# One weight unit made wholly resident in a segment-recurrent attention kernel, with its scratch homes shared

## The chip, the core and the metric

The kernel runs on one core of a Trainium2 chip. Its engines are TensorE (PE in the profile, with its weight loads as PEld), VectorE (DVE), ScalarE (ACT), GpSimd (POOL) and SyncE (SP); 16 DMA engines move data between HBM and the on-chip memory SBUF. TensorE accumulates in PSUM, which has eight banks. The metric is the device time of one execution in microseconds (us), as the median of several runs.

## The reference

Two branches read the same normalised rows `xn` of `x` (2048 rows of 1024): a feed-forward branch with a GELU over 3584 columns, and an attention that walks through the rows in 64 segments of 32, each together with eight memory rows. The first eight output rows of a segment are the memory of the next, so the segments form a chain.

```python
def _A_ref(x, mem0, Wq, Wk, Wv, Wo, seg_len):
    ...
    for s in range(n_seg):
        xs = x[:, s * seg_len:(s + 1) * seg_len, :].copy()
        h = jnp.concatenate([mem, xs], axis=1)
        q = jnp.einsum('btd,dhe->bhte', h, Wq)
        k = jnp.einsum('btd,dhe->bhte', h, Wk)
        v = jnp.einsum('btd,dhe->bhte', h, Wv)
        scores = jnp.einsum('bhqe,bhke->bhqk', q, k) * scale
        scores = jnp.where(mask[None, None], scores, -1000000000.0)
        p = _softmax(scores, axis=-1)
        o = jnp.einsum('bhqk,bhke->bhqe', p, v)
        o = jnp.einsum('bhte,hed->btd', o, Wo)
        mem = o[:, :M, :].copy()
        outs.append(o[:, M:, :])
    return jnp.concatenate(outs, axis=1)
...
xn = _layernorm(x, axis=-1)
return x + _A_ref(xn, ...) + _B_ref(xn, B_w1, B_b1, B_w2, B_b2)
```

There are 32 heads of 128. Each of the four weights Wq, Wk, Wv and Wo has 1024 x 4096 elements of bf16.

## The kernel before

**Phases.** The first 416 us compute the normalised rows, their transposes and the whole feed-forward branch, and put `x` plus that branch back to HBM as a residual (`R_n`, and from there, laid out for the segments, into the second half of `hr_d` and `hrL_d`). Then the segment loop runs 64 times.

**Units.** The attention's weights are cut into 64 units of 128 x 2048 elements (512 KB). A segment takes them in the order of `pass_order`: half passes K0, Q0, K1, Q1, V0, V1 of eight units each (0 and 1 are the two halves of the heads), then pass O with 16. A unit of the six half passes is four matmuls of 512 columns side by side, one in each group of 32 columns of the array (`product`, L774); pass O is `o_product` (L1010).

**Resident and streamed.** 46 units lie in SBUF for good, in places that the feed-forward branch gave up (`RES_PLACES`), in the `late` pool (`LATE`), or in `xt2` and `xt3`. 18 units (an "S" in `PLACED`) are streamed again in each segment through a ring of six slots (`RING`). When a streamed unit is done, `unit_done` calls `start_stream`, which fills the freed slot with the next unit in order. Three of the 18 are special. `IN_PSUM` (the second streamed unit of Q0) and `IN_BANKS` (the last unit of pass O) are kept in four PSUM banks and copied to their slot by DVE (L271, two instructions of 512 words each); they are started three places late (`LATER`). `PART` is the streamed unit third from the end of the streamed units of pass O (O's unit 11): its first 1792 of 2048 columns lie in `half_home`, and only 256 columns (512 B in each of 128 rows, 64 KB) are streamed into its slot (L282). All other transfers of a unit are whole (L284). SP issues them all.

**The scores.** Within a segment the attention of head half `u` is: `scores(u)` on TensorE into the bank `mixed` (L884, L890), `exps(u)` (ACT's Exp into `pr`, L899, then two masks on DVE, L906), `sums(u)` (sums on TensorE L914 and L920, then Ln and two Exp on ACT, L925 and L928, then two products on DVE, L937 and L941, into `pdA` and `pdB`), and `values(u)` on TensorE (L956, L962) with four copies out (L975). They are put between the units of later half passes by unit number: `scores(0)` after the last unit of K1, `sums(0)` after unit 4 of Q1 (`SUMS_0`), `scores(1)` with `exps(1)` after unit 0 of V1 (`ATTEND`), `values(0)` around unit 4 of V1, `sums(1)` after unit 5 or 6 of V1, and `values(1)` after unit 5 of O. The queries of both halves use one home, `q_home` (a view of `q_all`): `turn_q` copies them out of PSUM with ACT (L826) and transposes them in place with DVE (L840). `q_left` puts the queries of left rows beside them (L862).

**Homes.** `pr_all` holds pr of both halves. `pdB` of half 0 lies in `res_home`, the second half of `hr_home`; `pdB` of half 1 at the end of `q_all`. `hr_home` also receives the rows of the next segment (first half) and the residual of the running one (second half): from segment 6 on one transfer of 1 KB rows brings both, behind V1 (L293, on POOL). Before that, ACT issues the two separately.

**Left rows.** Each segment owns 24 rows and its eight memory rows in the main products; eight "left" rows of four segments each are collected and computed together. So the segments differ by `i4 = s % 4`: left keys in the K passes, left queries in Q and left values in V are added in some of them, and in those with `i4 == 1` (`left_o`) pass O has the left rows as well. `left_outs` and `left_keys` are interleaved in two homes, `ko_flat`.

**The end of a segment.** `put_mem` (L320, L330) turns the first output rows into the next segment's memory rows; then DVE adds the residual (L1178), and the output goes out with four small transfers (L1213), from POOL from segment 5 on. All engines run their instructions in program order; dependences become semaphore waits.

Of the kernel before, what the change touches and what calls it, by code (L numbers as in the profile page):

```python
# [10 lines left out]
BF16 = mybir.dt.bfloat16  # L11
# [35 lines left out]
STREAMED = 18  # L47
# [16 lines left out]
AT_BANKS, AT_PART = 5, 3  # L64
PART_COLS = 1792


def pass_order():
# [15 lines left out]
    "S..S...." "S...S..." "S....S.." ".S.....S" "....S..." "S..S..S." "...S..S." "S..S..SS",  # L84
    "S..S...." "S...S..." "S....S.." ".S.....S" "....S..." "S..S..S." "...S..S." "S..S..SS",
    "S..S...." "S...S..." "S....S.." ".S.....S" "....S..." "S..S..S." "...S..S." "S..S..SS",
    "S..S...." "S...S..." "S....S.." ".S.....S" "....S..." "S..S..S." "...S..S." "S..S..SS",
# [21 lines left out]
IN_BANKS, PART = STREAMED_O[AT_BANKS], STREAMED_O[AT_PART]  # L109
# [5 lines left out]
def kernel(  # L115
# [34 lines left out]
    hr_d = dram.tile([NSEG + 1, P, 512], BF16, name="hr_d")  # L150
    hrL_d = dram.tile([NGRP + 1, P, 512], BF16, name="hrL_d")
# [12 lines left out]

    half_home = nc.alloc_sbuf_tensor_at("half_home", [P, PART_COLS], BF16, offset=SCRATCH)

    part_home = half_home[:, :]
# [5 lines left out]
    hr_home = consts.tile([P, 512], BF16, name="hr_home")  # L173
    res_home = hr_home[:, 256:512]
    pr_all = consts.tile([P, 224], BF16, name="pr_all")
    pd_main = consts.tile([P, 320], BF16, name="pd_main")
# [9 lines left out]
    qL_last = consts.tile([P, 16, SEG], BF16, name="qL_last")  # L186
    qL = [consts.tile([P, 16, SEG], BF16, name="qL"), qL_last]
    ident = res_home[:, 0:P]
    make_identity(nc, ident)
    ident_mem = nc.alloc_sbuf_tensor_at("ident_mem", [P, 4, NL], BF16, offset=SCRATCH + 2 * PART_COLS)  # L190
# [9 lines left out]
    mask = qL_last.rearrange("p h t -> p (h t)")[:, 0:NX + GRP * 16]  # L200
# [29 lines left out]
    for k in range(7):  # L230
# [8 lines left out]
        unit: dram.tile([P, 2048 - PART_COLS if unit == PART else 2048], BF16, name="Wc_" + "_".join(map(str, unit)))[:, :]  # L239
# [3 lines left out]
    def fetch(t, unit):  # L243
        w, i, u = unit
        if unit == PART:
            h = 4 * i + 2 * u
            nc.sync.dma_start(out=t, in_=Wo_v[:, h + 1, PART_COLS - DM:])
        elif w == "O":
# [24 lines left out]
    def start_stream(slot):  # L273
# [7 lines left out]
        elif unit == PART:  # L281
            nc.sync.dma_start(out=t[:, PART_COLS:], in_=copies[unit])  # L282
# [8 lines left out]
    def load_x_rows(s, eng=nc.sync):  # L291
        n = 512 if s > 5 else 256
        eng.dma_start(out=hr_home[:, 0:n], in_=hr_d[s, :, 0:n])  # L293
        nxt["hT"] = hr_home[:, 0:256].rearrange("p (k t) -> p k t", k=KT)

    def load_left_rows(g, eng=nc.sync):
        hr = hrp.tile([P, 256], BF16, name="hrL")
        eng.dma_start(out=hr[:, :], in_=hrL_d[g, :, 0:256])
# [6 lines left out]
    ko_flat = [d_oL[:, 512:], sp.tile([P, 16 * 48], BF16, name="ko1")[:, :]]  # L305
    ko = [t.rearrange("p (h t) -> p h t", h=16) for t in ko_flat]
    left_outs, left_keys = [t[:, :, 0:SEG] for t in ko], [t[:, :, 2 * NL:] for t in ko]
    q_all = sp.tile([P, 640], BF16, name="q_all")
# [28 lines left out]
    with tc.tile_pool(name="ma", bufs=2) as ma, tc.tile_pool(name="mps", bufs=6, space=PSUM) as mps:  # L337
# [95 lines left out]
        def keep_xT(tg, xnT):  # L433
            xl = [t[:, 0:512].rearrange("p (g k i t) -> p g k i t", g=2, k=KT, i=GRP) for t in ko_flat]
            for half in range(2):
                nc.sync.dma_start(
                    out=hr_d[16 * tg:16 * tg + 16, :, 128 * half:128 * half + 128].rearrange("s p c -> p s c"),
# [7 lines left out]
            for k in range(2):  # L445
                nc.sync.dma_start(
                    out=hrL_d[4 * tg + 2 * k:4 * tg + 2 * k + 2, :, 0:256].rearrange("g p c -> p g c"),
# [15 lines left out]
        def turn_R(ttg, eng, small=None):  # L463
# [3 lines left out]
            for i in range(4):  # L467
# [4 lines left out]
                    t[:, 256:512].rearrange("(h r) c -> r h c", h=2)  # L472
                    for t in (hr_d[min(4 * og + 1, NSEG - 1) + 1, :, :], hrL_d[og, :, :])
# [5 lines left out]
                else:  # L479
                    pairs = [(hr_d[seg + 1, :, 256:512].rearrange("(j t) c -> t j c", j=4), rows)]  # L480
# [69 lines left out]
        for tg in range(4):  # L550
            last = tg == 3
            if last:
# [4 lines left out]
                nc.sync.dma_start(out=half_home[:, 0:DM], in_=Wo_v[:, h, :])  # L557
# [122 lines left out]
    with tc.tile_pool(name="late", bufs=1) as late, \  # L680
# [67 lines left out]
        for s in range(NSEG):  # L748
# [101 lines left out]
            def turn_q(ps):  # L850
                turn(ps, q_home[:, :, NL:40], nc.scalar.copy)
# [399 lines left out]
```

## Time and profile before

| what | value |
|---|---|
| median of 3 runs (lowest to highest) | 1830.54 us (1828.19 to 1836.0) |
| profiled execution, its own time | 1831.03 us |
| its span, instructions | 1828.9 us, 71537 |
| granted TensorE clock | 0.999 |
| busy PE, DVE, ACT, POOL | 1723.1, 959.5, 670.1, 269.3 us |
| moved by DMA | 596.27 MB |
| first and last `put_mem` matmul (L320) | 449.9 and 1801.3 us |

Between the first and the last `put_mem` lie 62 segments. The page's slices divide the span in 40 equal parts of 45.7 us; the loop begins in the tenth. A wait line gives the engine and line that waited, what released it, and then the total in us, how often, and the longest. A timeline line gives start and length in us, engine, line, operation, output and input.

### The profile page before, as it was taken

The page shows a single profiled execution, that of the slowest core. Times are in us where ns is not written, and L with a number is a line of the kernel's source. Part 1 is how long each engine was busy: PE and PEld are TensorE (multiplying, and loading weights), DVE is VectorE, ACT ScalarE, POOL GpSimd, SP SyncE. Part 2 cuts the span into 40 slices and gives each one's busy share as a digit, 9 for nine tenths or more (in the row PEclk, how much of TensorE's full clock was granted, in tenths as well). Part 3 has the DMA queues.
Part 4 walks back from the last instruction along what each step waited for, and adds up shares of the span by engine and source line. Part 5 has one row for each costly group of instructions (what it writes and reads, how often), then busy time and mean ns, then how long its engine had stood idle before and what let it go on. Part 6 is the DMA issues. An engine that isn't in the chain of part 4 may idle for free.

```text
span 1828.9 us, 71537 instructions
## 1 busy us (share of the span) xinstructions
PE 1723.1 (94%) x31207; PEld 873.1 (48%) x31207; DVE 959.5 (52%) x2443; ACT 670.1 (37%) x1572; POOL 269.3 (15%) x526
## 2 busy tenths in 40 slices
PE   8999999998999999999999999999999999999987
PEld 4444444444444445454445544454444444445444
DVE  7657483805455545455555555555555454545544
ACT  5334251602333334333333333333333333333333
POOL 0000001501231111111111111111111111111111
PEclk9999999999999999999999999999999999999999
DMA  9931211769999999999999999999999999999997
GB/s 290 314 88 48 53 46 49 252 221 362 379 385 378 377 371 386 373 389 367 388 384 377 401 375 380 379 380 376 380 372 385 374 374 376 370 393 395 369 379 304
DMA packets 230662, 596.27 MB, mean 326 GB/s; under 512 B 46411, under 2 KB 86107, under 8 KB 230348
## 3 DMA queue, kind: packets, MB, share of 16 engines
q1 hardware_dynamic: 207028, 571.28, 83.8%
q0 software_dynamic: 15872, 16.44, 2.8%
q8 instruction: 244, 4.00, 0.9%
q10 hardware_dynamic: 7448, 3.98, 0.7%
q14 instruction: 70, 0.57, 0.1%
HBM read 577.63 MB, written 28.97 MB: 332 GB/s over the span
## 4 chain that ended last, share of the span: by engine, by line
PE 65%; DMA 30%; issue 2%; DVE 1%; ACT 1%; SPq 0%; ACTq 0%; POOL 0%; DVEq 0%; POOLq 0%
PE acc L774 29%; DMA u<-Wc_V 13%; PE ps L503 11%; PE acc L1010 10%; PE ps L624 8%; DMA u<-Wc_O 7%; DMA u<-Wc_Q 5%; DMA u<-Wc_K 3%; PE ps L657 2%; PE acc L956 2%; DMA hr_home<-hr_d 1%; DVE u L271 1%; PE pT L657 1%; PE mixed L320 0%; PE mixed L884 0%
## 5 line engine op out<-in xcount | busy, mean ns | idle before, releaser
L774 PE MATMUL acc<-u,hr_home 128*32 128x512 bf16 x11520 | 793.4, 380 | 52.7 <-DMA u<-Wc_V 24.7
L774 PEld LDWEIGHTS <-hr_home 128*32 128x32 bf16 x12288 | 327.9, 96 | 374.5 <-issue 70.2
L774 PE MATMUL acc<-u,hrL 128*32 128x512 bf16 x2880 | 250.4, 380 | 1.7 <-issue 1.5
L503 PE MATMUL ps<-u 128*128 128x512 bf16 (+1 forms) x920 | 195.7, 375 | 2.0 <-ACT u L423 2.0
L271 DVE TENSOR_SCALAR u<-kept 128x512 uint32<-128x512 uint32 x254 | 163.5, 685 | 60.0 <-PE acc L1010 38.3
L826 ACT CAST d_oL<-acc 128x512 bf16<-128x512 f32 x143 | 82.0, 586 | 270.5 <-PE acc L774 258.4
L624 PE MATMUL ps<-u 128*128 128x512 bf16 x672 | 147.0, 379 | 0.0
L503 PEld LDWEIGHTS <-u 128*128 128x128 bf16 x920 | 90.5, 99 | 105.4 <-issue 2.4
L1010 PE MATMUL acc<-u,q_all 128*32 128x256 bf16 (+1 forms) x2096 | 126.5, 301 | 14.7 <-DMA u<-Wc_O 10.9
L1010 PE MATMUL acc<-u,d_oL 128*32 128x512 bf16 x1944 | 133.6, 381 | 7.1 <-DMA u<-Wc_O 4.1
L937 DVE TENSOR_TENSOR pd_main<-pr_all,mixed 128x320 bf16<-128x320 bf16 x128 | 62.5, 488 | 126.9 <-ACT mixed L928 125.3
L830 ACT CAST q_all<-acc 128x512 bf16<-128x512 f32 x128 | 75.4, 589 | 144.1 <-PE mixed L890 141.0
L840 DVE STREAM_TRANSPOSE q_all<-q_all 128x512 bf16<-128x512 bf16 x128 | 90.6, 708 | 70.7 <-ACT q_all L826 70.7
L1010 PEld LDWEIGHTS <-q_all 128*32 128x32 bf16 x3381 | 102.0, 96 | 53.6 <-ACT q_all L975 23.2
L1213 POOL DMA_DIRECT2D out_dram<-hr_home x172 | 88.1, 512 | 243.1 <-DVE hr_home L1178 237.7
L293 POOL DMA_DIRECT2D hr_home<-hr_d x58 | 32.9, 567 | 594.9 <-PE acc L774 581.7
L826 ACT CAST q_all<-acc 128x512 bf16<-128x512 f32 x128 | 75.3, 589 | 93.4 <-PE acc L774 93.4
L774 PEld LDWEIGHTS <-hrL 128*32 128x32 bf16 x3072 | 83.4, 96 | 48.1 <-issue 2.8
L624 PEld LDWEIGHTS <-u 128*128 128x128 bf16 x672 | 65.3, 98 | 77.3 <-DVE g_u L585 0.4
L1010 PEld LDWEIGHTS <-d_oL 128*32 128x32 bf16 x2592 | 67.7, 96 | 62.6 <-issue 15.0
L928 ACT ACTIVATE mixed<-mixed,small_consts 128x160 f32<-128x160 f32 x256 | 94.4, 369 | 8.4
L577 ACT ACTIVATE g_xb<-ps,b1col 128x512 bf16<-128x512 f32 x112 | 76.9, 687 | 55.3 <-PE ps L503 54.5
(139 smaller groups left out, 2094.5 us busy)
## 6 DMA issues: line engine op xcount, KB each, us to landing
u<-Wc_K SPq DMA_DIRECT2D x256, 512.0 KB
u<-Wc_V SPq DMA_DIRECT2D x256, 512.0 KB
u<-Wc_O SPq DMA_DIRECT2D x256, 512.0 KB
u<-Wc_Q SPq DMA_DIRECT2D x192, 512.0 KB
u<-in_B_w_dram SPq DMA_DIRECT2D x28, 512.0 KB
hr_home<-hr_d POOLq DMA_DIRECT2D x58, 128.0 KB, 5.3
u<-in_A_Wq_dram SPq DMA_DIRECT2D x13, 512.0 KB
u<-in_A_Wv_dram SPq DMA_DIRECT2D x12, 512.0 KB
```

Source lines behind the costliest of these rows:

```text
L271: nc.vector.tensor_single_scalar(out=out, in_=in_, scalar=0, op=ALU.bitwise_or)
L503: nc.tensor.matmul(ps[:, SEG * s0:SEG * s1].rearrange("p (s t) -> p s t", t=SEG), lhsT=w1_sb[fb // 2][:, kt, (fb % 2) * P:(fb % 2 + 1) * P ...
L577: nc.scalar.activation(out=xb[:, :], in_=ps[:, :], func=ACT.Identity, bias=b1col[:, fb:fb + 1], scale=1.0)
L624: nc.tensor.matmul(ps[:, :], lhsT=gts[fc // 4][:, fc % 4, t * P:(t + 1) * P], rhs=w2_sb[fc // 2][:, fc % 2, cs], start=(fc == 0), stop=(fc ...
L774: nc.tensor.matmul(o, lhsT=lhs[:, i, :], rhs=m, start=(i == seq[0]), stop=(i == seq[-1]), tile_position=(0, 32 * j),)
L826: cp(out=out, in_=ps.rearrange("p (h e) -> p h e", e=32))
L830: cp(out=t[:, :], in_=ps[:, :])
L840: nc.vector.transpose(out=home, in_=home)
L928: nc.scalar.activation(out=mixed[:, 160 * b:160 * b + 160], in_=mixed[:, 0:160], func=ACT.Exp, scale=-1.0, bias=off[:, b:b + 1],)
L937: nc.vector.tensor_tensor(out=pdA.rearrange("p c b q -> p b c q"), in0=prA[:, None, :, :].to_broadcast([P, 2, 4, 40]), in1=dd, op=ALU.mult,)
L1010: nc.tensor.matmul(acc[r0:r0 + rows, c:c + wide], lhsT=lhsT, skip_group_check=True, rhs=cols, start=start, stop=stop, tile_position=(0, r0),)
L1213: eng.dma_start(out=out_flat[rows, 256 * j:256 * j + 256], in_=res[32 * j:32 * j + NX, :])
```

## The change

O's unit 11 becomes resident as a whole: `STREAMED` is 17, the "S" at its place in `PLACED` becomes ".", it gets a place of its own in the `late` pool, and `PART`, `part_home` and the split of its columns in `o_columns` go. `IN_BANKS` is still the last unit of O. The 512 B in each partition come from sharing homes:

- `hr_home`, both `qL` and `pd_main` lie where `half_home` was; `pr_all` is gone.
- pr of half 0 lies in columns 400 to 623 of `q_all`, where the second queries will be; pr of half 1 lies in `res_home`.
- So `q_left(1)` moves from within `exps(0)` to behind `sums(0)`, and the copy of the second queries is cut in two at head 10 (column 400 of `q_all`).
- `pdB` of half 0 lies in a strided part of `left_outs`; its product is made in two instructions.
- The residual has DRAM tensors of its own (`res_d`, `resL_d`) and is loaded by itself after unit 0 of O, behind the products of `sums(1)`; the rows (`rows_d`, `rowsL_d`) are loaded where they were.
- `ko1` and `q_all` become parts of one tile `kq`, which also receives half of the banked unit at the start.

```diff
-STREAMED = 18
+STREAMED = 17
...
-AT_BANKS, AT_PART = 5, 3
-PART_COLS = 1792
+AT_BANKS = 4
...
-    "S..S...." "S...S..." "S....S.." ".S.....S" "....S..." "S..S..S." "...S..S." "S..S..SS",
+    "S..S...." "S...S..." "S....S.." ".S.....S" "....S..." "S..S..S." "...S..S." "S.....SS",
...
-    half_home = nc.alloc_sbuf_tensor_at("half_home", [P, PART_COLS], BF16, offset=SCRATCH)
+    hr_home = nc.alloc_sbuf_tensor_at("hr_home", [P, 512], BF16, offset=SCRATCH)[:, :]
+    qL = [
+        nc.alloc_sbuf_tensor_at(f"qL{u}", [P, 16, SEG], BF16, offset=SCRATCH + 1024 * (u + 1))[:, :, :] for u in range(2)
+    ]
+    pd_main = nc.alloc_sbuf_tensor_at("pd_main", [P, 320], BF16, offset=SCRATCH + 3072)[:, :]
...
-        elif unit == PART:
-            nc.sync.dma_start(out=t[:, PART_COLS:], in_=copies[unit])
...
     def load_x_rows(s, eng=nc.sync):
-        n = 512 if s > 5 else 256
-        eng.dma_start(out=hr_home[:, 0:n], in_=hr_d[s, :, 0:n])
+        eng.dma_start(out=hr_home[:, 0:256], in_=rows_d[s, :, :])
...
-            def turn_q(ps):
-                turn(ps, q_home[:, :, NL:40], nc.scalar.copy)
+            def turn_q(ps, cuts=(0, 16)):
+
+                for h0, h1 in zip(cuts, cuts[1:]):
+                    nc.scalar.copy(
+                        out=q_home[:, h0:h1, NL:40], in_=ps[:, 32 * h0:32 * h1].rearrange("p (h e) -> p h e", e=32)
+                    )
+                let_go(ps)
+                home = q_home[:, :, NL:40]
+                nc.vector.transpose(out=home, in_=home)
...
-            def exps(u, meanwhile=None):
+            def exps(u):
 
-                pr = pr_all[:, 0:224]
+                pr = res_home[:, 0:224] if u else q_all[:, 400:624]
...
-                if meanwhile is not None:
-                    meanwhile()
...
-                pdB = (q_all[:, 512:640] if u else res_home[:, 0:128]).rearrange(
-                    "p (c b a q) -> p c b a q", c=4, b=2, q=NL
-                )
+                if u:
+                    pdB = q_all[:, 512:640].rearrange("p (c b a q) -> p c b a q", c=4, b=2, q=NL)
+                else:
+                    c0 = 0 if first else NL * slot
+                    pdB = left_outs[1 if first or i4 >= 2 else 0][:, :, c0:c0 + NL].rearrange(
+                        "p (c b a) q -> p c b a q", c=4, b=2
+                    )
...
+                else:
+                    for a in range(2):
+                        nc.vector.tensor_tensor(
+                            out=pdB[:, :, :, a, :].rearrange("p c b q -> p b c q"),
+                            in0=prB[:, None, :, NL * a:NL * a + NL].to_broadcast([P, 2, 4, NL]),
+                            in1=dd[:, :, :, 32 * a:32 * a + NL], op=ALU.mult,
+                        )
...
-            exps(0, None if first else lambda: q_left(1))
+            exps(0)
...
-            if not first:
-                at[SUMS_0[i4]] = [lambda: sums(0)]
+            at[7 if first else SUMS_0[i4]] = [lambda: sums(0)] + ([] if first else [lambda: q_left(1)])
...
-            turn_q(psQ1)
+            turn_q(psQ1, (0, 10, 16))
...
             def load_res():
                 st["res"] = res_home
-                if s < 5:
-                    nc.scalar.dma_start(out=res_home, in_=hr_d[s + 1, :, 256:512])
+                (nc.scalar if s < 5 else nc.gpsimd).dma_start(out=res_home, in_=res_d[s + 1, :, :])
...
             if not final:
                 load_x_rows(s + 1, nc.scalar if s < 5 else nc.gpsimd)
-            else:
-                nc.gpsimd.dma_start(out=res_home, in_=hr_d[s + 1, :, 256:512])
```

More of the change, by code (lines that the diff above doesn't have):

```diff
@@ L244, in fetch @@
         w, i, u = unit
[L245 to L248, printed above, removed]
+        if w == "O":
             h = 4 * i + 2 * u
```

100 lines of the change are left out of this document (45 added, 55 removed).

## The prediction

> **What bounds the kernel now.** I read the page's slices first, then its chain, then the waits of TensorE, then windows of 1 us, and last the timeline of one segment. The slices show the 16 DMA engines at nine tenths or more all through the segment loop (from slice 10 on), at 367 to 401 GB/s in most slices; the chain that ended last runs through TensorE and, for nearly a third of the span, through the transfers of streamed weights.
>
> ```profile
> DMA  9931211769999999999999999999999999999997
> GB/s 290 314 88 48 53 46 49 252 221 362 379 385 378 377 371 386 373 389 367 388 384 377 401 375 380 379 380 376 380 372 385 374 374 376 370 393 395 369 379 304
> ...
> PE 65%; DMA 30%; issue 2%; DVE 1%; ACT 1%; SPq 0%; ACTq 0%; POOL 0%; DVEq 0%; POOLq 0%
> ```
>
> The waits of TensorE (total us, times, longest) are few and small, and nearly all are for streamed units:
>
> ```profile
> PE acc L774 <- DMA u<-Wc_V: 24.7, 56, 1.8
> PE acc L1010 <- DMA u<-Wc_O: 15.0, 28, 1.4
> PE acc L774 <- DMA u<-Wc_Q: 11.6, 19, 1.7
> PE acc L774 <- DMA u<-Wc_K: 4.3, 7, 1.7
> ```
>
> That is 55.6 us, the most that a better stream can give. The loop is balanced: some 62 segments in 1351 us (21.8 us each), with under 1 us of DMA wait in each. I call a segment s of kind s mod 4. Kind 1 projects the left rows in pass O as well; there TensorE is slow and the ring fills. The windows (the last two columns are DMA share and GB/s) cross from a kind 1 into the next segment:
>
> ```profile
> 1165.00:1166.00 1.00, 1.00 (x28) 0.49 (x20) 0.35 (x2) 0.25 (x1) 0.57 (x1) 1.00 1.03 397
> ...
> 1167.00:1168.00 1.00, 1.00 (x26) 0.65 (x22) 0.45 (x1) 0.00 (x0) 0.00 (x0) 1.00 0.95 332
> 1168.00:1169.00 1.00, 1.00 (x28) 0.48 (x20) 0.00 (x0) 0.00 (x0) 0.00 (x0) 1.00 0.93 299
> 1169.00:1170.00 1.00, 1.00 (x23) 0.36 (x16) 0.00 (x0) 0.59 (x1) 0.00 (x0) 1.00 0.79 274
> ...
> 1179.00:1180.00 1.00, 1.00 (x24) 0.57 (x17) 0.53 (x2) 0.59 (x1) 0.00 (x0) 1.00 1.03 422
> ```
>
> For about ten of each 87 us (four segments) the transfers are short of work and TensorE is the bound; in the rest the transfers are, and TensorE meets their delay in V, O and Q.
>
> **Part 1, the bytes.** In each of segments 1 to 63 the 64 KB of the partly resident unit are not streamed; in segment 0 the same 512 KB are fetched either way. 65,536 B at 380 GB/s are 0.17 us. The queue table gives the same from the other side:
>
> ```profile
> q0 software_dynamic: 15872, 16.44, 2.8%
> ...
> q10 hardware_dynamic: 7448, 3.98, 0.7%
> ```
>
> The ACT queue's packets average 534 B and take 0.007 x 1828.9 x 16 / 7448 = 27.5 ns; the POOL queue's average 1036 B and take 51.6 ns. The 128 rows of 512 B that go are 128 x 27.5 / 16 engines = 0.22 us. The residual loaded apart turns 128 rows of 1 KB into 256 of 512 B: 128 x (55.0 - 51.6) / 16 = 0.03 us more, and no more bytes. So 0.17 to 0.19 us; I take 0.17, and 63 x 0.17 = 10.7 us, of which 77/87 fall where transfers bind: **-9.5 us**. Bounds: -13.9 (0.22 everywhere) and 0 (TensorE the bound throughout).
>
> **Part 2, the ring.** With 17 places in the stream and six slots, a start happens when the unit six places before is done. The dropped place stands third from the end of pass O, so between the last unit of V0 and that place every start moves one streamed unit forward: the first of K1 starts when O's unit 8 is done and not at unit 11. The SP queue shows that start and the two before it:
>
> ```profile
> 1161.49 2.36 SPq L284 DMA_DIRECT2D u<-Wc_K  x2
> 1165.29 0.32 SPq L284 DMA_DIRECT2D u<-Wc_Q  x1
> 1167.47 1.60 SPq L284 DMA_DIRECT2D u<-Wc_K  x2
> ```
>
> Three units of O take some 1.3 us in kind 1 (the PE timeline steps 0.43 us a unit), so the start at 1167.47 comes at 1166.1, and the Q before it at about 1163.3. In the three windows from 1167 the engines moved 332, 299 and 274 GB/s and not 410, 0.33 MB or 0.8 us short. Half of that, 0.4 us in each of 16 rounds, is **-6.4 us**; bounds -13 and 0. Where transfers bind anyway, an earlier start only queues earlier. The copy of the banked unit on DVE also moves, from O's unit 8 to unit 6: 1.29 us of DVE work, in an idle stretch of DVE behind the two casts of `values`, costs nothing; were that cover gone it would delay the fold of L1031, which has until the end of O.
>
> **Part 3, the second queries' transposition.** pr of head half 0 now lies in q_all, so `q_left(1)` and the second piece of Q1's copy wait for `sums(0)`: Ln and two Exp on ACT, then the products on DVE. The timeline of a kind 1 before the change:
>
> ```profile
> 1156.50 0.59 ACT L826 CAST q_all<-acc 128x512 bf16<-128x512 f32 x1
> 1156.61 0.49 DVE L937 TENSOR_TENSOR pd_main<-pr_all,mixed 128x320 bf16<-128x320 bf16 x1 [0.94 <-ACT mixed L928]
> 1157.02 0.28 DVE L941 TENSOR_TENSOR hr_home<-pr_all,mixed 128x128 bf16<-128x128 bf16 x1
> 1157.21 0.70 DVE L840 STREAM_TRANSPOSE q_all<-q_all 128x512 bf16<-128x512 bf16 x1
> 1157.97 0.20 PE L884 MATMUL mixed<-q_all,d_oL 128*32 128x40 bf16 x4
> ```
>
> ACT's copy lay beside the products; the transposition followed them at once and ended at 1157.91, and `scores(1)` came 0.06 us later. Now: L941 for u = 0 becomes two instructions of 64 elements (DVE casts of 128x64 take 0.22 us and such pairs overlap by 0.08): 0.36 for 0.28, so +0.08. Then ACT's second piece, 192 columns: 0.21 us for 64 and 0.38 for 256 in L975's rows give 0.32. The overlap of 0.09 between product and transposition is lost, and two handovers come in at some 0.04 (ACT's end to DVE's start was 0.02 in L826 to L840 of Q0). Together +0.57 us on the transposition; if the piece also waits for `q_left(1)`'s copy (0.15), +0.72. Behind the waiting piece on ACT is only V0's copy, which needs `scores(1)` itself; behind the transposition on DVE the masks of pr(1). TensorE waits for both.
>
> Over all segments the transposition ended before `scores(1)` by, in the median, 1.57 us in kind 0, 0.30 in kind 1, 0.69 in kind 2 and 0.38 in kind 3. Taking 0.57 less each segment's own slack, where that is positive, gives 8.7 us over the loop; 2.1 of it stands within 4 us ahead of a DMA wait that it only replaces. Of the 6.6 left I take **+6 us**; bounds 0 (the stream absorbs it) and 14 (0.72, nothing absorbed).
>
> **Part 4, the residual.** It was in one transfer with the rows, behind V1. Now POOL issues it after the products of `sums(1)`, since pr(1) lies in its home. This row gives the landing:
>
> ```profile
> hr_home<-hr_d POOLq DMA_DIRECT2D x58, 128.0 KB, 5.3
> ```
>
> In kinds 0 and 3 those products end 4.3 us before `put_mem`, the add of L1178 stands 0.5 us after it: the data is late by about 0.5 us; in kind 2 by nothing, in kind 1 it is 2 us early. DVE has 0.35 us idle before the bank copy of L271 and 0.84 before K0's transposition, which cover it: **0 us**, bounds 0 and +6 (0.2 us in each of 31 segments). The Trainium skill, page "DMA: Bandwidth & Descriptors", section "Rules for kernel authors", speaks against this edit: many small transfers should be one large one. Its section "Anatomy of one DMA" fits 2.0 us plus bytes over 436 GB/s for this path, an estimate of 2.2 us for 64 KB; by it the residual would land ahead of its add everywhere and the bound of +6 would fall away. This trace has 5.3 us, so I keep it.
>
> The added issue (0.57 us, L293) lies in POOL's idle time; the piece of PART that PE read in two matmuls in kind 1, and the memory moves, change nothing on the path. POOL's row load goes before the residual, so put_mem's rows aren't later.
>
> **Sum.** -9.5 - 6.4 + 6 + 0 = -9.9 us on the profiled 1831.0 (0.5 above the median 1830.5, span 1828.9 and 2.1 around it): **1820.6** on the median.
>
> **Rivals.** *The stream opens up:* parts 1 and 2 near their bounds (10.7 + 13) and 2 us of stall left: 1809. For it: 55.6 us of DMA wait, most at V, just behind `scores(1)`. Against: the starts in K and Q don't move. *The attention chain becomes the bound (slower):* in V1 of kinds 1, 2 and 3, `scores(1)` waits for the transposition 0.72 us later, 13.5 us of stall, and with TensorE the bound neither byte nor start counts: 1844. It decides from 0.25 us of stall per segment (15.9 / 63). For it: slack of 0.06 us above. Against: mean PE busy is 20.6 of 22.0 us and DMA share about 1.0. *The change does nothing:* the 9.5 us are eaten by 6 of stall and 3 of late residual, and the dip of part 2 stays because the two banked units leave the transfers idle there: about 1830.
>
> **Chances.** Forecast 0.46 (its own range 1813 to 1828), open stream 0.16, attention chain 0.24, nothing 0.14. A difference under 0.5% (9.2 us) is not told from none: faster is below 1821.4, slower above 1839.7. A bit over half the forecast (0.26) and the open stream: 0.42. Slower: nearly all of the chain's case, 0.22. Same: 0.36. The range 1805 to 1845 cuts the lower part of the second case and half of the third.
>
> **What would show it.** Part 1: no transfer of 64 KB from Wc_O, and some 0.17 us less per segment where TensorE waits on V and Q. Part 2: windows around the end of pass O of kind 1 above 332 GB/s. Part 3: a second ACT cast of 192 columns that starts after L941's successor, and waits of `scores(1)` on DVE, 0.2 us now in all, near 9 us. Part 4: waits of L1178 on the residual's DMA, and no bank copy behind it that makes TensorE wait. Waits of TensorE for DVE or ACT above 16 us, with waits for DMA falling no further, would prove the forecast wrong.

## The result, and the profile after

In a common comparison of twenty runs each, the kernel before takes 1835.81 us in the median (1827.66 to 1841.41) and the changed one 1827.69 (1821.98 to 1837.09). The ratio is 0.9962, with a 95% interval of 0.9947 to 0.9978: 7.0 us less, 4.0 to 9.7 by the interval. The three runs of before that the forecast started from had 1830.54, which lies 5.3 us below the median of twenty; from there the changed kernel is only 2.9 us lower. The profiled execution after took 1824.59 us, with a span of 1822.9.

The page of the changed kernel, its DMA row in 40 slices and what its engines moved:

```profile
DMA  9931211769999999999999999999999999999997
GB/s 287 315 91 48 54 46 46 251 221 367 386 374 373 372 360 386 369 377 380 372 375 381 382 380 391 359 383 380 375 378 393 369 390 383 392 377 384 377 386 282
...
DMA packets 222215, 592.08 MB, mean 325 GB/s; under 512 B 46283, under 2 KB 77531, under 8 KB 221900
...
PE 63%; DMA 21%; issue 6%; DVE 5%; ACT 4%; POOL 0%; ACTq 0%; SPq 0%; DVEq 0%; POOLq 0%
```

4.19 MB fewer are moved (596.27 before), which is 64 times 64 KB: 63 streamed pieces, and the one transfer that laid their copy down in HBM at the start. The DMA engines are as full as before, but on the chain that ended last their share falls from 30% to 21%, and what they lose goes to DVE, ACT and "issue". TensorE's waits (total us, times, longest) say the same:

```profile
PE acc L1015 <- DMA u<-Wc_O: 12.8, 27, 1.3
PE acc L1015 <- issue: 10.6, 17, 1.6
PE mixed L884 <- DVE kq L851: 10.6, 29, 0.5
PE acc L767 <- issue: 10.5, 15, 2.1
PE acc L767 <- DMA u<-Wc_V: 5.8, 15, 0.9
PE acc L966 <- DVE pd_main L939: 5.3, 21, 0.3
...
PE acc L767 <- DVE u L266: 4.7, 8, 1.4
PE acc L767 <- DVE hr_home L1176: 4.5, 6, 1.5
PE acc L767 <- DVE hr_home L323: 3.8, 11, 0.6
...
PE acc L767 <- DMA u<-Wc_K: 0.7, 3, 0.3
```

The waits for streamed units fall from 55.6 to 19.3 us, and the one for Wc_Q is gone. But most of that comes back in other waits. The five DVE rows shown add up to 28.9 us, and the same five causes were 6.6 before (L884 0.2, L956 3.8, L330 2.2, L271 0.4, L1178 nothing): 22.3 more. "Issue", in which nothing that the profile shows was waited for, rises from 17.9 to 31.4 us over all of TensorE's lines.

### The profile page after: what moved, and what is told of

Same layout as the page of the kernel before. It is cut to its first block, busy times and chain, and to the rows that moved or that the text cites. A ratio compares the mean times of both kernels' runs of the same rounds, so it can differ in the third digit from the quotient of the medians.

```text
span 1822.9 us, 71697 instructions
## 1 busy us (share of the span) xinstructions
PE 1715.6 (94%) x31153; PEld 886.1 (49%) x31173; DVE 972.1 (53%) x2507; ACT 678.0 (37%) x1636; POOL 300.3 (16%) x584
## 4 chain that ended last, share of the span: by engine, by line
PE 63%; DMA 21%; issue 6%; DVE 5%; ACT 4%; POOL 0%; ACTq 0%; SPq 0%; DVEq 0%; POOLq 0%
PE acc L767 28%; PE ps L496 10%; PE acc L1015 9%; PE ps L617 8%; DMA u<-Wc_O 5%; DMA u<-Wc_V 5%; DMA u<-Wc_K 3%; DMA hr_home<-res_d 3%; DMA hr_home<-rows_d 2%; PE ps L650 2%; ACT mixed L926 2%; PE acc L966 1%; DVE u L266 1%; DMA pd_main<-resL_d 1%; DVE kq L851 1%
## 5 line engine op out<-in xcount | busy, mean ns | idle before, releaser
L767 PEld LDWEIGHTS <-hr_home 128*32 128x32 bf16 x12288 | 336.2, 96 | 334.7 <-issue 51.1
L266 DVE TENSOR_SCALAR u<-kept 128x512 uint32<-128x512 uint32 x254 | 162.8, 683 | 1.6 <-PE acc L767 0.8
L1015 PEld LDWEIGHTS <-kq 128*32 128x32 bf16 x3908 | 103.3, 96 | 73.8 <-ACT kq L985 22.5
L851 DVE STREAM_TRANSPOSE kq<-kq 128x512 bf16<-128x512 bf16 x128 | 91.1, 712 | 68.0 <-ACT kq L846 65.9
L846 ACT CAST kq<-acc 128x512 bf16<-128x512 f32 (+2 forms) x192 | 85.3, 444 | 113.0 <-PE acc L767 83.1
L1015 PE MATMUL acc<-u,kq 128*32 128x256 bf16 (+1 forms) x2372 | 114.7, 312 | 12.2 <-DMA u<-Wc_O 9.2
L285 POOL DMA_DIRECT2D hr_home<-rows_d x58 | 32.7, 564 | 536.4 <-PE acc L767 536.4
L823 ACT CAST kq<-acc 128x512 bf16<-128x512 f32 x128 | 75.2, 588 | 110.5 <-PE mixed L890 109.9
L570 ACT ACTIVATE g_xb<-ps,b1col 128x512 bf16<-128x512 f32 x112 | 76.8, 686 | 55.6 <-PE ps L496 54.7
L966 PEld LDWEIGHTS <-kq 64*128 64x128 bf16 x1024 | 42.4, 95 | 71.7 <-ACT kq L823 39.0
```

The lines of the kernel that those rows point to most:

```text
L266: nc.vector.tensor_single_scalar(out=out, in_=in_, scalar=0, op=ALU.bitwise_or)
L570: nc.scalar.activation(out=xb[:, :], in_=ps[:, :], func=ACT.Identity, bias=b1col[:, fb:fb + 1], scale=1.0)
L767: nc.tensor.matmul(o, lhsT=lhs[:, i, :], rhs=m, start=(i == seq[0]), stop=(i == seq[-1]), tile_position=(0, 32 * j),)
L823: cp(out=t[:, :], in_=ps[:, :])
L846: nc.scalar.copy(out=q_home[:, h0:h1, NL:40], in_=ps[:, 32 * h0:32 * h1].rearrange("p (h e) -> p h e", e=32))
L851: nc.vector.transpose(out=home, in_=home)
```

## Where the time went in the trace

**The dip behind kind 1 stayed, and the other kinds opened.** The three windows of the forecast, by the same clock times (the last two columns are DMA share and GB/s):

```profile
1167.00:1168.00 1.00, 1.00 (x22) 0.47 (x19) 0.78 (x2) 0.00 (x0) 0.00 (x0) 1.00 1.04 393
1168.00:1169.00 1.00, 1.00 (x28) 0.52 (x21) 0.00 (x0) 0.00 (x0) 0.00 (x0) 1.00 1.06 381
1169.00:1170.00 1.00, 1.00 (x24) 0.56 (x20) 0.00 (x0) 0.00 (x0) 0.00 (x0) 1.00 1.00 361
```

332, 299 and 274 GB/s seem to have become 393, 381 and 361. But the segment runs 1.5 us later here: its first `put_mem` matmul starts at 1171.45, not at 1169.93. The last 3 us ahead of that matmul, before and then after:

```profile
1166.95:1169.95 3.00, 3.00 (x63) 1.44 (x52) 0.50 (x1) 0.59 (x1) 0.00 (x0) 1.00 0.90 305
```

```profile
1168.45:1171.45 3.00, 3.00 (x59) 1.44 (x47) 0.00 (x0) 0.58 (x1) 0.54 (x1) 1.00 0.86 306
```

The dip has only moved with the segment. Over the 16 segments of kind 1 these 3 us have 321 GB/s in the mean before and 303 after, though the first start of K1 comes 3.8 us ahead of `put_mem` and not 2.5, the 1.3 us that were forecast. A table over segments 1 to 62, worked out from the traces, shows where the stream did open. The rate is that of the last 7 us ahead of `put_mem`, the length goes from one `put_mem` to the next, and `r1_ring_back` is a run below in which the ring's starts are put back:

| kind (segments) | GB/s before | in `r1_ring_back` | changed | length before, us | in `r1_ring_back` | changed |
|---|---|---|---|---|---|---|
| 0 (15) | 359 | 327 | 385 | 21.48 | 22.06 | 21.30 |
| 1 (16) | 354 | 356 | 347 | 23.15 | 23.26 | 23.40 |
| 2 (16) | 395 | 381 | 410 | 21.00 | 21.00 | 20.58 |
| 3 (15) | 340 | 310 | 384 | 21.52 | 22.00 | 21.45 |

Each column is one execution; the lengths are good to some 0.2 us. In kind 1, the only one for which part 2 counted a gain, neither the rate nor the length got better. The rate rose in kinds 0, 2 and 3.

**The queries' chain** of the same kind 1 (start and length in us, then engine, line and operation):

```profile
1157.84 0.43 ACT L846 CAST kq<-acc 128x320 bf16<-128x320 f32 x1
1157.95 0.49 DVE L939 TENSOR_TENSOR pd_main<-kq,mixed 128x320 bf16<-128x320 bf16 x1 [0.85 <-ACT mixed L926]
1158.36 0.35 DVE L951 TENSOR_TENSOR d_oL<-kq,mixed 128x64 bf16<-128x64 bf16 x2
1158.74 0.32 ACT L846 CAST kq<-acc 128x192 bf16<-128x192 f32 x1 [0.47 <-DVE d_oL L951]
...
1159.09 0.71 DVE L851 STREAM_TRANSPOSE kq<-kq 128x512 bf16<-128x512 bf16 x1 [0.15 <-ACT kq L846]
...
1159.85 0.20 PE L884 MATMUL mixed<-kq,d_oL 128*32 128x40 bf16 x4
```

From the start of the first product to the transposition there are 1.14 us, and there were 0.60: 0.54 later, where 0.57 were forecast. Two products of 64 columns take 0.35 (0.36 forecast), the second piece 0.32 (0.32). `scores(1)` now follows the transposition and waits 10.6 us in all (near 9 forecast).

**The residual and its companion.** DVE's add at the end of a segment now waits for two transfers:

```profile
DVE hr_home L1176 <- DMA hr_home<-res_d: 61.4, 46, 2.8
...
DVE pd_main L1176 <- DMA pd_main<-resL_d: 17.6, 11, 2.7
```

Before, these were 4.8 us in 4 waits and 2.1 us in 4. The second one I had not looked at. In kind 1 pass O has left rows, whose residual `resL` is a further POOL transfer. POOL's timeline in the same kind 1 of the changed kernel:

```profile
1163.40 0.57 POOL L285 DMA_DIRECT2D hr_home<-rows_d  x1 [10.95 <-PE acc L767]
1165.40 0.56 POOL L1104 DMA_DIRECT2D hr_home<-res_d  x1 [1.43 <-DVE kq L944]
1170.00 0.54 POOL L1142 DMA_DIRECT2D pd_main<-resL_d  x1 [4.04 <-issue]
```

and before:

```profile
1162.18 0.56 POOL L293 DMA_DIRECT2D hr_home<-hr_d  x1 [11.70 <-PE acc L774]
1165.18 0.57 POOL L1144 DMA_DIRECT2D pd_main<-hrL_d  x1 [2.43 <-DVE ko L975]
```

The third transfer (it was the second) goes out 6.6 us behind the rows, not 3.0, after 4 us in which POOL waits for nothing that the profile names. The rows, issued at 1163.40, take this long to land:

```profile
DMA to landing us min/median/max: 6.3/6.3/6.3
```

So they land at 1169.67, 0.33 us ahead of the third issue. That is no accident: in each of the twelve traces in which POOL issues rows, residual and `resL` one behind the other, `resL` goes out 0.33 us behind the landing of the rows in all 15 rounds that have the three (180 in all). Its instruction waits for no semaphore of the rows' transfer, so it is not the program that ties the two. What it holds up is seen on DVE, then on TensorE:

```profile
1174.67 0.42 DVE L1176 TENSOR_TENSOR pd_main<-acc,pd_main 128x256 bf16<-128x256 f32 x1 [2.70 <-DMA pd_main<-resL_d]
1175.01 0.41 DVE L1176 TENSOR_TENSOR hr_home<-acc,hr_home 128x256 bf16<-128x256 f32 x1
```

```profile
1175.48 0.83 PE L767 MATMUL acc<-u,hr_home 128*32 128x512 bf16 x12 [1.50 <-DVE hr_home L1176]
```

In kind 1 the add reads pass O's sums straight from their PSUM bank (`psX`). The bank is free only behind both adds, and Q0's first product of the next segment needs it: 1.5 us of TensorE.

## The experiments

All ratios are to the kernel before, with 95% intervals.

**The two homes, undone one by one.** `c0_control` is the changed kernel with its left rows' products made from columns of a resident weight, which frees 512 B per partition. The others give pr of half 0, of half 1, or of both such a home (`pr_own`), and undo the wait that the shared home makes.

```diff
-        eng.dma_start(out=hr[:, :], in_=rowsL_d[g, :, :])
+        eng.dma_start(out=spare_d[g % 2, :, :], in_=rowsL_d[g, :, :])
...
-                pr = res_home[:, 0:224] if u else q_all[:, 400:624]
+                pr = pr_own[:, :]
...
-            at[7 if first else SUMS_0[i4]] = [lambda: sums(0)] + ([] if first else [lambda: q_left(1)])
+            at[7 if first else SUMS_0[i4]] = [lambda: sums(0)]
...
-            turn_q(psQ1, (0, 10, 16))
+            turn_q(psQ1)
...
+            load_res()
```

> The changed kernel with the left rows' products made from a resident weight's columns instead of the loaded left rows (whose load goes to a spare HBM tensor), so that 512 B in each partition are free; the left rows' results are not those of the reference. Both theories: the time of the changed kernel, 0.996 of the kernel before. It is the control for the next three.

> The control with pr of half 0 in a home of its own: q_left(1) back in exps(0), the second queries' copy in one piece, no wait for the products of sums(0). Theory A (the stream binds, TensorE's other waits are mostly absorbed): 0 to 4 us under the control, and TensorE's waits for DMA grow by what the 10.6 us of waits of scores(1) shrink. Theory B (the attention chain and the late residual bind now): 8 to 14 us under the control, waits for DMA grow by less than 3 us.

> The control with pr of half 1 in a home of its own, so that the residual is loaded directly behind the rows and waits for no product. Theory A: 0 to 2 us under the control, as my sum had it (0 us for the residual). Theory B: the waits of L1176 on the residual (61.4 us on DVE) and TensorE's waits for DVE behind it (4.7 for the bank copy, 4.5 for the add) go, 6 to 12 us under the control.

> The control with one home of its own for pr of both halves, both edits above at once: only the bytes, the ring and the residual's separate transfer remain of the change. Theory A: 2 to 6 us under the control. Theory B: the two sums add up, 14 to 24 us under the control, about 0.985 of the kernel before.

Measured: 0.9967 [0.9943, 0.9992] for the control, 0.9945 [0.9924, 0.9967] with the queries' part undone, 0.9984 [0.9964, 1.0003] with the residual loaded early again, 0.9940 [0.9919, 0.9962] with both. Undoing part 3 gains 0.0022 beside the control and 0.0044 beside `a4_own_pr1`, in the mean 6 us (2 to 10 by the intervals): the forecast's +6. The residual's wait on pr(1) is worth nothing that can be seen. But in `a34_own_pr`, where rows and residual go out one behind the other, `resL` is late all the same: DVE waits 20.1 us for it in 14 rounds. So it is not pr's wait that makes it late.

**Fewer bytes in the kernel before.** Only 32 of the 128 rows of `PART`'s last columns are streamed and multiplied.

```diff
-            nc.sync.dma_start(out=t[:, PART_COLS:], in_=copies[unit])
+            rows = P if n < STREAMED else 32
+            nc.sync.dma_start(out=t[0:rows, PART_COLS:], in_=copies[unit][0:rows, :])
```

> The kernel before with only 32 of the 128 rows of PART's streamed columns fetched from segment 1 on, and the matmuls on those columns contracting over these 32 rows (part of the contraction is left out): 48 KB per segment less, the ring and everything else as before. If the gain of the change is its bytes: 0.75 of part 1, 7 to 8 us under the kernel before. If it is the ring's earlier starts: under 2 us.

Measured: 1.0072 [1.0055, 1.0090], slower. This says nothing of the bytes, since the edit disturbs TensorE:

```profile
PE 1743.8 (95%) x31207; PEld 870.5 (47%) x31207; DVE 959.5 (52%) x2443; ACT 669.2 (36%) x1572; POOL 268.5 (15%) x526
```

Its busy time is 1743.8 us against 1723.1 before, and a segment of kind 1 lasts 24.17 us, against 23.15.

**The bytes given back.** In the changed kernel, 64 KB are moved in each segment from one DRAM tensor to another, at O's unit 11.

```diff
+                if n == 11 and not first:
+                    nc.sync.dma_start(out=spare_d[s % 2, :, :], in_=rows_d[s, :, :])
```

> The changed kernel with a transfer of 64 KB from HBM to a spare HBM tensor, issued by SP behind O's unit 11 in each segment from 1 on: the bytes are back, the ring's starts stay early. If the gain is the bytes: the ratio goes back to 1.000 to 1.003 of the kernel before (9 to 11 us over the changed kernel). If it is the ring: within 2 us of the changed kernel, 0.996.

Measured: 0.9992 [0.9972, 1.0012], 0.0030 above the changed kernel: 5.5 us (1 to 10). The bytes are worth a little more than half of the 9.5 forecast, though the interval reaches up to it; the 64 KB here go between DRAM tensors, which is near to the old transfer but not the same.

**`resL` from ACT.** In the changed kernel, the third transfer leaves POOL's queue; `f2_loads_act` moves the rows and the residual there too.

```diff
-                    (nc.scalar if s < 5 else nc.gpsimd).dma_start(
-                        out=st["resL"], in_=resL_d[og, :, :]
-                    )
+                    nc.scalar.dma_start(out=st["resL"], in_=resL_d[og, :, :])
```

> The changed kernel with the left rows' residual (resL, once in four segments) issued by ACT and not by POOL. In the changed kernel POOL issues it 3 to 4.6 us behind the residual, with nothing shown that it waits for, as if a third transfer of 128 rows had no room on its queue until the rows had landed; DVE then waits up to 2.7 us for it, and TensorE at the start of the next segment for DVE (0.28 us at the add, 0.08 at the bank copy). If the queue is the cause, the wait of L1176 for resL (17.6 us) goes. If TensorE's waits decide: 4 to 6 us under the changed kernel; if the stream absorbs them: 0 to 2 us.

> The same with the rows and the residual of all segments issued by ACT as well. If the 5.3 us to landing belong to POOL's path, the rows and the residual land 1 to 3 us earlier, the waits of L1176 (61.4 us) and L323 for transfers go, and the time is 3 to 8 us under the changed kernel. If the landing is set by the transfers queued on the same 16 engines, nothing changes by more than 2 us, and ACT's issues (0.33 us each) stand before L985's copies.

Measured: `f1_resL_act` 0.9931 [0.9905, 0.9957], 1819.20 us, 5.7 us below the changed kernel by the ratios (an interval of some 0 to 11). The timeline of POOL, and that of ACT's queue, in the same kind 1:

```profile
1161.25 0.55 POOL L1104 DMA_DIRECT2D hr_home<-res_d  x1 [1.44 <-DVE kq L944]
...
1161.86 0.32 ACTq L1142 DMA_DIRECT2D pd_main<-resL_d  x1
```

0.6 us behind the residual and not 4.6, and the wait on DVE is 1.5 us, not 17.6; TensorE no longer waits for the add in kind 2:

```profile
DVE pd_main L1174 <- DMA pd_main<-resL_d: 1.5, 3, 0.7
```

`f2_loads_act` is 0.9985 [0.9955, 1.0016], worse than `f1_resL_act` and not told apart from the changed kernel: rows that ACT issues come later.

```profile
PE acc L767 <- DVE hr_home L323: 20.3, 30, 2.1
...
DVE hr_home L323 <- DMA hr_home<-rows_d: 42.1, 34, 2.8
```

DVE waited 12.9 us for the rows in the changed kernel, and TensorE 3.8 for `put_mem`.

**The ring as it was.** In the changed kernel, the slot of V1's first streamed unit is held back until O's unit 11, so that every start between is one place later, as before. The start at unit 11 itself is not held so long: the slot has been free for a while, and the trace has it 0.4 us behind the start before it (in a kind 1, 4.3 us ahead of `put_mem` and not 2.5). `rd_ring_and_bytes_back` has the 64 KB of `d1_dummy_64k` as well.

```diff
+            if unit == HELD_TO:
+                start_stream(held.pop())
             if IS_STREAMED[unit]:
-                start_stream(slot_of.pop(place_in_stream.pop(unit)))
+                slot = slot_of.pop(place_in_stream.pop(unit))
+                if unit == HELD_FROM:
+                    held.append(slot)
+                else:
+                    start_stream(slot)
```

> The changed kernel with the ring's starts put back: the slot that V1's unit 0 frees stays empty until O's unit 11 is done, so each start from V1's unit 3 on comes one streamed unit later, as in the kernel before; the 64 KB stay away. d1_dummy_64k put the bytes at about 5.5 us of the 7 that the change won. If the ring is worth what is left and what the homes cost (5 to 7 us, near my 6.4): ratio 0.999 to 1.001. If the earlier starts are worth nothing: 0.996 to 0.997.

> Both put back: the starts as in r1_ring_back and the spare 64 KB transfer of d1_dummy_64k. Only the shared homes and the residual's own transfer remain. If part 3 costs 4 to 6 us and part 4 nothing (as a3_own_pr0 and a4_own_pr1 showed): 1.002 to 1.004 of the kernel before. If the homes cost nothing: 1.000 or below.

Measured: 1.0092 [1.0077, 1.0107] and 1.0130 [1.0113, 1.0147]. The starts are worth 0.0130 of the changed kernel, 24 us, nearly four times the 6.4 forecast; the bytes on top of that another 7 us. In `r1_ring_back` Q's wait is back, and the wait for the late add doubles:

```profile
PE acc L777 <- DMA u<-Wc_Q: 11.7, 23, 1.6
...
PE acc L777 <- DVE hr_home L1186: 8.9, 10, 2.1
```

The forecast counted only the dip behind kind 1. Pass O of a kind 0 has one too. Windows of 3.5 to 3.7 us in pass O of a kind 0, in `r1_ring_back` and then in the changed kernel, same segment:

```profile
1239.10:1242.80 3.70, 3.41 (x84) 1.91 (x84) 1.57 (x7) 2.22 (x8) 0.56 (x1) 1.00 0.94 329
1242.80:1246.40 3.60, 3.47 (x86) 2.01 (x78) 2.98 (x7) 1.16 (x4) 0.56 (x1) 1.00 0.95 308
```

```profile
1228.80:1232.30 3.50, 3.10 (x68) 1.50 (x61) 1.76 (x7) 2.36 (x8) 0.95 (x2) 1.00 1.05 399
1232.30:1235.80 3.50, 2.89 (x76) 1.99 (x75) 2.38 (x5) 0.73 (x2) 0.17 (x1) 1.00 1.01 394
```

Single segments differ (another kind 0 of the changed kernel shows 327 and 360), and the table above has the means. By its lengths the starts are worth 0.76, 0.42 and 0.55 us in each segment of kinds 0, 2 and 3, some 26 us in all, and nothing in kind 1 (2 us the other way): that makes up the 24 us. Part of kind 2's share is the late add, which the row above has twice as dear.

**Shifts around `scores(1)`.** `g1_sums_earlier` is `f1_resL_act` with `sums(0)` a unit earlier; `g2_scores_later` also has `scores(1)` and `values(0)` a unit later in kinds 1 to 3.

```diff
-SUMS_0 = (4, 4, 4, 4)
+SUMS_0 = (3, 3, 3, 3)
...
-ATTEND = (0, 0, 0, 0)
+ATTEND = (0, 1, 1, 1)
```

> f1_resL_act with sums(0) one unit earlier in Q1 (SUMS_0 3 for 4), so that the second piece of the queries' copy is released 0.2 us earlier. If the transposition's delay is what part 3 costs: TensorE's wait of scores(1), 8.4 us in f1_resL_act, falls to 2 to 4 us, and the time by 1 to 4 us: 0.990 to 0.993. If the sums then wait for pr's masks on DVE: no gain, and waits of L912 above 3 us.

> g1_sums_earlier with scores(1) one unit later in V1 in kinds 1, 2 and 3 (ATTEND 1 for 0) and values(0) one unit later there. The wait of scores(1) goes to under 1 us. If nothing is late behind it: 0.989 to 0.992. If values(1) in pass O then wait for the products of sums(1), which come 0.2 us later: no better than g1_sums_earlier, with more waits of L966.

Measured: 0.9933 [0.9911, 0.9955], 1819.64 us, and 1.0013 [0.9994, 1.0033]. The wait of `scores(1)` falls from 8.4 us in `f1_resL_act` to 4.7 in `g1_sums_earlier`, and the time stays. In `g2_scores_later` the products of half 1 are late for `values(1)` instead:

```profile
PE acc L966 <- DVE pd_main L939: 25.3, 34, 1.5
```

**Everything back but the transfers.** On `rd_ring_and_bytes_back`: pr of both halves in a home of its own (`ra_all_back`), or of one half (`r3_ring_back_own_pr0`, `r4_ring_back_own_pr1`), with the edits of the first group.

> a34_own_pr (homes of their own for pr, residual loaded behind the rows, left rows from a resident weight) with the ring's starts and the 64 KB put back as in rd_ring_and_bytes_back. If the held slot stands truly for PART's: 0.999 to 1.002 of the kernel before, and the homes cost 20 us or more when the starts are late. If holding the slot costs by itself: 1.008 to 1.012, and the ring is worth no more than some 6 us.

> ra_all_back, but only pr of half 0 in a home of its own (the queries' chain as before the change, the residual late). If the residual's lateness makes most of the difference between ra_all_back and rd_ring_and_bytes_back: within 4 us of rd. If the queries' chain does: within 4 us of ra.

> ra_all_back, but only pr of half 1 in a home of its own (the residual early, the queries' chain late). The other way round: near ra if the residual's lateness makes the difference, near rd if the queries' chain does.

Measured: 1.0069 [1.0045, 1.0092], 1.0079 [1.0061, 1.0096] and 1.0080 [1.0049, 1.0110]. `ra_all_back` should have been as fast as before and is 0.7% slower. One thing of the change it still has: the residual is a transfer apart.

```profile
PE acc L778 <- DVE hr_home L1191: 13.3, 12, 2.4
...
DVE pd_main L1191 <- DMA pd_main<-resL_d: 30.6, 15, 3.6
```

The add waits 30.6 us for `resL`, against 2.1 before, with the residual issued as early as the rows. That speaks for the third transfer. The held slot may cost something of its own, but not much: `p34_homes_alone` below has the homes of `rd_ring_and_bytes_back` without a held slot, and the latter is only 0.0022 above it (-0.0016 to 0.0060). The other two runs don't decide between the residual and the queries: both lie near `ra_all_back` and some 9 us below `rd_ring_and_bytes_back`, so with late starts either edit alone gains nearly all that both gain.

**The add put off.** On `g1_sums_earlier`: the residual's add and the output go behind unit 1 of the next K0, so that DVE is free for `put_mem` and the bank copy first.

```diff
-            let_go(psX)
+            if not left_o:
+                let_go(psX)
...
+            tails.append(tail)
...
-            psK, psKL = half_pass("K", 0, left_k[0], {})
+            psK, psKL = half_pass("K", 0, left_k[0], {1: [tails.pop()]} if tails else {})
```

> g1_sums_earlier (resL on ACT, sums(0) one unit earlier) with the residual's add and the output's transfers put behind unit 1 of the next segment's K0, so that the bank copy of L266 and K0 do not stand behind a late residual on DVE. If TensorE's waits behind the late residual (bank copy 0.5 to 4 us, put_mem's copy 5.3 us in g1) come from it: 2 to 6 us under g1_sums_earlier, 0.990 to 0.992. If they come from the rows' own landing: within 2 us of it.

Measured: 0.9981 [0.9962, 1.0001], 9 us above `g1_sums_earlier`. TensorE waits for the add after nearly every kind 1, and a segment of kind 2 lasts 21.12 us, not 20.11:

```profile
PE acc L768 <- DVE hr_home L1180: 8.4, 15, 0.7
```

A later add holds `psX`'s bank longer: the same path as that of the late `resL`, here by the edit.

**The parts alone, on the kernel before.** `p3_queries_alone` has part 3 (pr of half 0 in `q_all`, the cut copy, `q_left(1)` behind `sums(0)`); `p34_homes_alone` also has part 4 (pr of half 1 in `res_home`, the residual by itself). Eighteen streamed places and all bytes stay.

```diff
-                pr = pr_all[:, 0:224]
+                pr = res_home[:, 0:224] if u else q_all[:, 400:624]
...
-        n = 512 if s > 5 else 256
+        n = 256
...
+                (nc.scalar if s < 5 else nc.gpsimd).dma_start(out=res_home, in_=hr_d[s + 1, :, 256:512])
```

> The kernel before with part 3 alone: pr of half 0 in q_all, q_left(1) behind sums(0), the second queries' copy in two pieces. The forecast had +6 us (bounds 0 and 14): 1.0033 of the kernel before. If the stream absorbs the delay: 1.000 to 1.001. If late starts make it dear, as r3 and r4 against rd hint: 1.005 or more.

> The kernel before with parts 3 and 4: pr of half 1 in res_home and pdB of half 0 in left_outs besides, rows and residual in transfers of their own. The forecast had +6 and 0 us and 0.03 us of packets per segment (2 us): 1.003 to 1.004, and then bytes and ring together won 13 to 14 us of my 15.9. If the homes cost 11 us, as rd against ra: 1.006, and bytes and ring won 18. If they cost nothing: 1.000, and bytes and ring won 7.

Measured: 1.0025 [1.0004, 1.0045] and 1.0108 [1.0073, 1.0142]. Part 3 costs 4.6 us. Part 4 costs 0.0083 more, some 15 us (8 to 23), where I had put 0 with a bound of +6.

```profile
PE acc L773 <- DVE hr_home L1192: 10.9, 9, 3.0
...
DVE hr_home L1192 <- DMA hr_home<-hr_d: 57.5, 44, 3.8
...
DVE pd_main L1192 <- DMA pd_main<-hrL_d: 26.9, 15, 4.2
```

TensorE did not wait for the add at all before the change; here it does, up to 3.0 us at a time, and a segment of kind 2, the one behind the left rows' add, lasts 21.99 us, not 21.00: in 16 such segments, 16 of the 27 us by which this execution is the longer one.

## Why the prediction went wrong

The direction was right and the size too large: -9.9 us forecast, -7.0 [-9.7, -4.0] in the common comparison, -2.9 if counted from the three runs that the forecast started from. With less than 0.5% it is the case "not told from none", where faster had been the likeliest. Some of that is the base, and no step of mine: three runs, 5.3 us below the median of twenty. That the sum came as near as it did is luck: the errors of parts 2 and 4, some 18 and 15 us, nearly cancel. By its steps:

1. **Part 4 failed: "late by about 0.5 us; in kind 2 by nothing, in kind 1 it is 2 us early", "0 us".** Alone on the kernel before it costs some 15 us; in the changed kernel, moving `resL` off POOL gives back 5.7 (0 to 11). The step counted when the residual lands, and POOL's time as idle ("the added issue lies in POOL's idle time"), but not what comes behind it on the same queue: in kind 1 the residual is now second and `resL` third, which goes out only when the rows have landed, 6.6 us behind their issue and not 3.0. Nor did it follow the add past DVE. I named the bank copy and K0's transposition as cover; the add also holds a PSUM bank. Without that lateness the change stands at 0.9931, 12.7 us below before. The residual itself was sized too small as well (61.4 us of wait in 46 segments, 1.3 us each, not 0.5), but that costs little: with early starts, undoing its wait gains nothing.
2. **Part 2 failed in its place: "half of that, 0.4 us in each of 16 rounds", -6.4 us.** The 16 rounds are the ends of kind 1, and there the earlier starts bring nothing: the dip is as deep as before (303 GB/s for 321) and the segment no shorter (23.40 us for 23.15). What was put at nothing, "Where transfers bind anyway, an earlier start only queues earlier", is where the gain lies: in kinds 0, 2 and 3 the last 7 us ahead of `put_mem` move 385, 410 and 384 GB/s, and 327, 381 and 310 with the starts put back, which costs 24 us. The DMA share of the 40 slices, at nine tenths or more, hides those dips. Late starts also make the late add dearer (L1186's 8.9 us for 4.5). Why the dip of kind 1 stays is open.
3. **Part 1, -9.5 us: likely too large.** 5.5 (1 to 10) in the changed kernel, 7 with late starts; 9.5 is not ruled out. The bytes did vanish; which waits take the rest of the gap no run shows.
4. **Part 3, +6 us: right** in size (4.6 alone, 6 undone) and in the delay (0.54 us for 0.57). That TensorE pays for it in the wait of `scores(1)` is only half shown: the wait is 10.6 us in the changed kernel, but 2.1 in `p3_queries_alone`, and in `g1_sums_earlier` it falls by 3.7 without any gain.
5. **The sum was not a sum.** Parts 1 and 2 over `p34_homes_alone` are worth 0.0146, 27 us (20 to 34); with parts 3 and 4's waits undone, as in `a34_own_pr`, they bring 11 (7 to 15) against the kernel before, with `resL` still late; 15.9 were forecast. Early starts seem to cover what the late residual would cost, so that each is worth more where the other is bad: with late starts, undoing parts 3 and 4 gains 11 us (`ra_all_back` below `rd_ring_and_bytes_back`), with early ones 5 (`a34_own_pr` below the control). -27 + 15 + 4.6 = -7 closes by construction, since each run is the next one's base; what it shows is that two terms were not the -15.9 and 0 that I had.

Of the rivals, *the attention chain becomes the bound* has its place right and its price not: 10.6 us of wait, not 13.5 with every gain lost. *The stream opens up* is what the DMA waits did (55.6 to 19.3), and yet the time did not follow, since DVE and "issue" waits rose by 22.3 and 13.5. *The change does nothing* has both of its causes borne out in part: the late residual, and "the dip of part 2 stays" (its reason, the two banked units, was not tried). But the time did move: its 0.5 us are further from the measured 7.0 than the forecast's 9.9.

Of the signs listed, those of parts 1 and 3 are there, except that the 0.17 us a segment of part 1 can't be told from the rest of the fall on V and Q. That of part 2 is there only by the clock: in windows that end with `put_mem` it is not (303 GB/s, where above 332 was asked). That of part 4, "no bank copy behind it that makes TensorE wait", is not: the wait for L266 rose from 0.4 us to 4.7. The waits for DVE went above 16 us, as the last sign of a wrong forecast has it, though those for DMA fell on.

Open: what it is in POOL's queue that lets the third transfer go only when the first has landed. That it does is shown (180 of 180 rounds); that the queue has room for two such transfers is likely, but no run fills it by itself. DVE, at least, isn't what holds it. This is all that DVE runs in the changed kernel between 1165.4 and 1171, and it ends 2.2 us before the transfer goes out at 1170.00:

```profile
1165.99 0.56 DVE L985 CAST kq<-acc 128x64 bf16<-128x64 f32 x2 [1.33 <-PE acc L972]
1166.49 1.29 DVE L266 TENSOR_SCALAR u<-kept 128x512 uint32<-128x512 uint32 x2
```

Nor is it known what the "issue" waits are.

The fastest versions seen are `f1_resL_act` and `g1_sums_earlier`, 1819.2 and 1819.6 us.

## What to carry to other kernels

Splitting a transfer costs not only its own landing: list everything issued behind it on that queue, with the consumer of each and the buffer or bank that this consumer holds, above all in the rare stage that has one transfer more. A wait that is cured in one engine is worth its full time only if the next one in line has slack; run the costs alone and the gains alone, since here some 27 us gained and 20 lost made 7. Read the GB/s of short windows in every kind of stage before a starting time is called worthless, and lay the windows of two kernels at the same instruction, not at the same clock time.

## What the runs showed of the hardware

The POOL queue in the changed kernel (KB, median us from issue to landing):

```profile
hr_home<-res_d POOLq DMA_DIRECT2D x59, 64.0 KB, 5.3
hr_home<-rows_d POOLq DMA_DIRECT2D x58, 64.0 KB, 5.5
...
pd_main<-resL_d POOLq DMA_DIRECT2D x16, 64.0 KB, 3.8
```

Half the bytes land no sooner: 128 KB took 5.3 us before. The Trainium skill, page "DMA: Bandwidth & Descriptors", section "Anatomy of one DMA", fits 2.0 us plus bytes over 436 GB/s, an estimate of 2.2 us for 64 KB. These rows disagree, beside a stream that fills the engines, and the measurement decides. The third transfer lands faster (3.8 us) but goes out later: 0.33 us behind the landing of the first of the three, 4.4 to 6.6 us behind its issue.

A DMA share near 1.0 is no full rate: in pass O it reads 0.94 and 0.95 at 329 and 308 GB/s in `r1_ring_back`, and 1.05 at 399 in the changed kernel.

In pass O of a kind 1 of `b1_fewer_bytes`, each of the two matmuls over 32 rows starts 0.31 us behind the matmul before it, and the next one 0.21 us later; around them, four matmuls over 128 rows start within 0.01 us of each other. A segment of kind 1 is 1.0 us longer there, with three quarters of the bytes of that piece gone.
